# Gate tiles per pair of strips, transposes in groups of eight, and a new TensorE order in a two-stage attention and gated convolution

## The chip, the cores and the metric

The kernel runs on one core of a Trainium2 chip. The metric is the device time of one execution in microseconds (us). The time shown is the median of three executions; beside it stands one profiled execution with its own time and its own span (first to last instruction).

## What is computed

The input `x` has 4 batches of 12800 rows of 128 channels, and 32 inducing rows attend to it; then the rows of `x` attend to the 32 results. A gated layer follows: a causal convolution of five taps gives a gate, a 128x128 product gives a value, and a second 128x128 product makes the output.

```python
def mab(q, kv):
    s = scale * (q @ kv.transpose(0, 2, 1))
    s = s - s.max(-1, keepdims=True)
    a = np.exp(s)
    a /= a.sum(-1, keepdims=True) + 1e-09
    return a @ kv
h = mab(I, x)                    # (4, 32, 128)
y = mab(x, h)                    # (4, 12800, 128)
for k in range(5):
    gate_pre += conv_w[k] * yp[:, k:k + S, :]   # yp: y with 4 zero rows ahead
gate = 1 / (1 + exp(-gate_pre))
out = (gate * (y @ w_val)) @ w_out
```

## The kernel before

**Tiling.** The 12800 rows of a batch are four strips of 3200 (`R = 4`), and 4 x 32 inducing rows fill the 128 partitions. Along a strip the work goes in chunks: eight in batch 0 (128 to 512 columns a strip), seven in each other batch (`SIZES`). `x` comes in twice: with channels on the partitions (`xt`, which the scores read) and with rows on the partitions (`xk`, which the weighted sums read). In batch 0 only chunk 4 of `xk` is loaded; the others are made on the chip from `xt` by TensorE transposes (`make_xk`, lines 379 to 413). For the other batches `xk` is loaded.

**Stages of a batch**, with the names that the order table uses:
- `s1` (line 425): scores of the inducing rows in float32, each strip in its own 32 columns of the array. VectorE copies them to `ss` and keeps the maximum (433).
- `gm` (437): the maximum over the chunks of a group (`GROUPS`) and over the strips (GpSimd, 453 to 460).
- `x` (379): in batch 0, 128x128 transposes in groups of four into PSUM, copied to `xk` by ScalarE (406) or VectorE (408) as `XEV` says.
- `h` (489): the exponentials (ScalarE, 468), transposed by VectorE (473), times `xk`; VectorE adds the sums up in `H` (498, 500).
- `u`, `t`, `w`, `W` (`prep` to `prep3`): the groups are put together and divided (`hn`, 539), transposed (`hT`, 548 to 551), turned into the gate and value weights in two float16 halves, and spread for the four strips (624, then copies 632 and 634).
- `s2` (694): scores of `x` against `hT`, and the softmax over 32 through VectorE (700, 705, 723 to 726, 740), GpSimd (711, 734) and ScalarE (717), ending in two float16 halves, `P1` (745) and `P2` (752).
- `r` (`rblock`, 781): a half block of the gated layer. Half 0 of chunk k ends the gates of strips 0 and 1, makes the values of chunk k-1 for strips 2 and 3 and begins chunk k's gates there; half 1 ends the gates of strips 2 and 3, makes chunk k's values for strips 0 and 1 and begins chunk k+1's gates there. A strip's gate has 15 matmuls (766), its value three (775); each uses 32 rows of the array, and the four strips run side by side. ScalarE then makes the `tanh` of a pair's gates (834), VectorE multiplies with the values (844), ScalarE and GpSimd split the product in float16 halves `gh` (857) and `gl` (862).
- `o` (`outp`, 866): three matmuls make a strip's outputs (880 to 882); ScalarE (892) or VectorE (890) copies them to `os`, as `OUTV` says, and SyncE stores them (897). The last chunk has one float32 product (873) instead.
- `z` (916): matmuls of zeros that fill a wait; eight more stand at the very start (905).

**PSUM.** Half of its eight banks is `a`, four buffers of one bank for everything but gates and transposes. The other half is one tile, `gates`, of four banks: bank r holds strip r's gates, and the groups of transposes of `x` use the four banks in turn.

**What sets the order.** TensorE goes through `ORDER`, a written table of the names above, from the front to the back. `Plan.order` (79) gives every operation the time by which its users need it and lays the other engines' queues out greedily, with costs from `COST` and shifts from `URGE`; `PASSES` says how often. The result is emitted as it stands. SyncE issues every load and store in one queue, in that order. Buffers are counted in `BUFS`: four tiles `xk`, eleven `xt`, four `os`.

Of the kernel before, what the change touches and what calls it, by code (L numbers as in the profile page):

```python
# [12 lines left out]
F32 = mybir.dt.float32  # L13
# [24 lines left out]
PASSES = 6  # L38
# [174 lines left out]
def tile_kernel(ctx: ExitStack, tc: tile.TileContext, xt, xk, indT_in, w64, out):  # L213
# [11 lines left out]
    gates = psum.tile([P, R, 512], F32, name="gates")  # L225
# [92 lines left out]
    def pt(key, shape=(P, 512), dt=F32):  # L318
        if key[0][0] == "g":
            t = st[key] = gates[:, int(key[0][1:])]  # L320
            return t
        t = st[key] = psum.tile(list(shape), dt, name=key[0], tag=key[0], bufs=BUFS[key[0]])
        return t
# [29 lines left out]
    def load_xt(b, c, u=1):  # L353
        n = wid(b, c)
        o = R * (FIRST[b][c] + (HALO if c else 0))
        key, at = xt_of(b, c, u)
        own = key[2] == c

        def f():
            if own:  # L360
                sb(pxt, key, [P, 16, R, 32])
            first = at - (HALO // 32 if c == 0 else 0)
            nc.sync.dma_start(st[key][:, first:first + n // 32].rearrange("p i r q -> p (i r q)"), xt[b, :, o:o + R * n])

        ix["xt", b, c, u] = sp(n * 2048 / BW + 1.2 * ((b, c) == (0, 2) and ("xt", 0, 1, 1) in ix), f, [key] * own, [key] * (not own))
# [13 lines left out]
    def make_xk(b, c, eng):  # L379
# [13 lines left out]
        for g in range(0, n, 4):  # L393
            k = min(4, n - g)
            tk = (f"g{g // 4 % 4}", "tp", b, c, g)

            def tp(g=g, k=k, tk=tk):
                t = st[tk] = pt(tk).rearrange("p (i c) -> p i c", c=P)
# [4 lines left out]
            def ev(g=g, k=k, tk=tk, e=eng[g // 4 % len(eng)]):  # L403
# [6 lines left out]
            e = eng[g // 4 % len(eng)]  # L410
            i = PE(0.109 * k + 0.02, tp, [ix["xt", b, c, 1], i_const], [tk], [xkey], lag=0.22)
            last.append(op("ACT" if e == "S" else "DVE", 0.6 if e == "S" else 0.69, ev, [i, i0], 0.0, [], [tk, key]))
# [347 lines left out]
    def gate_mm(b, c, r, u):  # L760
        if u == 0:
            pt((f"g{r}", b, c))
# [3 lines left out]
        T.matmul(st[f"g{r}", b, c][:, :n], st["W", b][q, w, k, :], st[("P1", "P2")[e]][q, o:o + n],  # L766
# [11 lines left out]
    seqs = [(b, c) for b in range(B) for c in range(len(SIZES[b]))]  # L778
    split = begun(tuple(SIZES[b][c] for b, c in seqs), len(taps), EVEN)

    def rblock(k, half):
# [20 lines left out]
        def part(whole):  # L802

            todo, new, use, before = [], [], list(held), max(spent.values())
            while any(work.values()) and (whole or any(w and w[0][0] is val_mm for w in work.values())):
# [4 lines left out]
                key = ("a", "v", b, c, r) if fn is val_mm else (f"g{r}", b, c)  # L810
                if u == 0:
                    new.append(key)
                elif key not in new and key not in use:
                    use.append(key)
# [13 lines left out]
        if cur:  # L828
# [3 lines left out]
            def th(b=b, c=c, p=p, n=SIZES[b][c]):  # L832
                t = sb(pw, ("tg", b, c, p), [P, 2, 512])
                S.activation(t[:, :, :n], gates[:, 2 * p:2 * p + 2, :n], AF.Tanh, scale=st["gsc", b])  # L834

            ix["tg", b, c, p] = op("ACT", cost("act", 2 * SIZES[b][c]) + 0.06, th, [i, ix["gsc", b]], 0.0, [("tg", b, c, p)],
                                   [(f"g{r}", b, c) for r in ends] + [("gsc", b)])
# [28 lines left out]
    def outp(k, r):  # L866
# [3 lines left out]
        key, os = ("a", "o", b, c, r), ("os", b, c, r)  # L870
        if k == len(seqs) - 1:
# [37 lines left out]
    def idle(k, n):  # L909

        key = ("g3", "idle", k)

        def f():
            t = pt(key)
# [40 lines left out]
GROUPS = [[[0, 1, 2], [3, 4], [5, 6, 7]], [[0, 1, 2, 3], [4, 5, 6]], [[0, 1, 2], [3, 4, 5, 6]], [[0, 1, 2], [3, 4, 5, 6]]]  # L955
ORDER = [
# [40 lines left out]
]  # L997
XEV = ["SSSS", "SSSS", "SVSS", "SSSS", "SSVS", "SSSV", "SVSS", "SSSV"]
URGE = {
    "e1.f": 2.5,  # L1000
    "s2.sub": 6,
    "s2.hi": -18.5,
    "s2.lo": 3.5,
    "s2.tout": 0,
    "s2.ex": 3,
    "s2.tin": -5,
    "rblock.gv": -4.5,
    "s2.sm": -7,
# [73 lines left out]
```

## Time and profile before

| | |
|---|---|
| median of three executions | 299.47 us (297.91 to 300.87) |
| the profiled execution | 299.25 us, of which the span is 297.1 us |
| granted TensorE clock | 0.997 |
| TensorE matmuls busy | 281.7 us, 95% of the span |
| VectorE, ScalarE, GpSimd busy | 228.1, 209.1, 213.6 us |
| HBM read, written | 47.63 MB, 26.21 MB |

In the chain of waits each piece has a start, a length and what ran. A matmul's row has its start and a modelled end, so the pace of TensorE is read from start to start. A float32 matmul of the scores or the weighted sums shows as two records.

### The profile page before, as it was taken

How to read it: one execution, taken by the hardware profiler on the slowest of the kernel's cores; microseconds unless marked ns; L12 is line 12 of the kernel's file. 1: busy time of each engine (PE TensorE's matmuls, PEld its weight loads, DVE VectorE, ACT ScalarE, POOL GpSimd, SP SyncE). 2: the span in 40 equal slices, each digit the busy share in tenths (PEclk: the TensorE clock that was granted, in tenths of full speed). 3: DMA queues.
4: the chain of work that ended last, by engine and by line, in shares of the span. 5: the costliest groups of instructions: out<-in, count | busy, mean ns of one | idle time of the engine just before them, and what ended most of it. 6: DMA issues, size and time to landing. Idle time of an engine off the chain costs nothing.

```text
span 297.1 us, 10038 instructions
## 1 busy us (share of the span) xinstructions
PE 281.7 (95%) x4040; PEld 136.8 (46%) x4040; DVE 228.1 (77%) x569; ACT 209.1 (70%) x325; POOL 213.6 (72%) x256
## 2 busy tenths in 40 slices
PE   8787799999999999999999999999999999999993
PEld 3454544565433435563544544464444344433442
DVE  1245599999795999896888888899888996786550
ACT  2372606378776859797588856958789698878784
POOL 1020117796975897889768897599999999997570
PEclk9999999999999999999999999999999999999998
DMA  7949999699993789989999593705243324333355
GB/s 294 425 176 365 389 382 410 227 330 388 342 332 145 221 319 353 410 270 334 347 399 340 163 354 112 277 3 195 89 166 120 129 109 155 133 139 145 143 212 188
DMA packets 24382, 74.50 MB, mean 251 GB/s; under 512 B 2832, under 2 KB 12560, under 8 KB 22160
## 3 DMA queue, kind: packets, MB, share of 16 engines
q1 hardware_dynamic: 24192, 73.84, 67.5%
q8 instruction: 32, 0.52, 0.7%
q14 instruction: 14, 0.11, 0.1%
q10 hardware_dynamic: 144, 0.02, 0.0%
HBM read 47.63 MB, written 26.21 MB: 249 GB/s over the span
## 4 chain that ended last, share of the span: by engine, by line
PE 80%; ACT 8%; DMA 5%; issue 3%; DVE 2%; SPq 1%; ACTq 0%; DVEq 0%
PE gates L766 26%; PE a L880 7%; PE a L489 7%; PE a L694 7%; PE a L425 6%; PE a L881 6%; PE a L882 6%; PE a L775 5%; DMA xt<-in_xt_dram 5%; PE gates L401 4%; PE gates L916 3%; ACT tg L834 2%; ACT gh L857 2%; ACT xk L406 2%; ACT os L892 2%
## 5 line engine op out<-in xcount | busy, mean ns | idle before, releaser
L862 POOL TENSOR_TENSOR gl<-tg,gh 128x1024 f16<-128x1024 f32 (+4 forms) x56 | 106.3, 1904 | 17.1 <-ACT gh L857 12.4
L766 PE MATMUL gates<-P,W 32*128 32x448 f16 (+5 forms) x1740 | 109.5, 345 | 1.2 <-ACT tg L834 1.1
L834 ACT ACTIVATE tg<-gates,gsc 128x1024 f32<-128x1024 f32 (+5 forms) x58 | 57.8, 996 | 34.9 <-PE gates L766 34.0
L844 DVE SCALAR_TENSOR_TENSOR tg<-tg,a 128x512 f32<-128x512 f32 (+5 forms) x116 | 65.4, 603 | 15.9 <-PE a L775 13.9
L766 PEld LDWEIGHTS <-W 32*128 32x128 f16 x1740 | 53.2, 92 | 42.5 <-issue 13.6
L857 ACT CAST gh<-tg 128x1024 f16<-128x1024 f32 (+4 forms) x56 | 52.6, 944 | 1.1 <-PE a L881 0.8
L892 ACT ACTIVATE os<-a,osc 128x448 f32<-128x448 f32 (+5 forms) x75 | 44.7, 616 | 8.1 <-PE a L882 4.1
L775 PE MATMUL a<-P,W 32*128 32x512 f16 (+5 forms) x348 | 42.4, 348 | 0.0
L880 PE MATMUL a<-gh,wo 128*128 128x512 f16 (+4 forms) x112 | 40.2, 359 | 0.0
L881 PE MATMUL a<-gh,wo 128*128 128x512 f16 (+4 forms) x112 | 39.6, 354 | 0.0
L882 PE MATMUL a<-gl,wo 128*128 128x512 f16 (+4 forms) x112 | 39.5, 354 | 0.0
L890 DVE TENSOR_SCALAR os<-a,osc 128x512 f32<-128x512 f32 (+3 forms) x41 | 27.8, 688 | 9.9 <-PE a L882 9.7
L752 POOL TENSOR_TENSOR P<-pt,P 128x512 f16<-128x512 f32 (+4 forms) x29 | 29.8, 1034 | 3.9 <-ACT P L745 3.7
L711 POOL TENSOR_TENSOR e<-e,m 128x512 f32<-128x512 f32 (+4 forms) x29 | 27.0, 938 | 6.6 <-DVE m L705 6.5
L734 POOL TENSOR_TENSOR e<-e,z 128x512 f32<-128x512 f32 (+4 forms) x29 | 27.1, 938 | 4.0 <-DVE z L726 1.5
L433 DVE TENSOR_SCALAR_CACHE_REDUCE ss<-a 128x512 f32<-128x512 f32 (+5 forms) x29 | 17.5, 605 | 15.0 <-PE a L425 14.6
L425 PE MATMUL a<-xt,indT 128*32 128x512 f32 (+5 forms) x232 | 27.6, 546 | 0.9 <-DMA xt<-in_xt_dram 0.8
L489 PE MATMUL a<-xk,et 128*32 128x129 f32 x800 | 27.9, 275 | 0.0
L489 PEld LDWEIGHTS a<-xk,et 128*32 128x32 f32 x800 | 23.2, 109 | 7.5 <-issue 5.0
L694 PE MATMUL a<-xt,hT 128*32 128x512 f32 (+4 forms) x232 | 26.5, 545 | 0.0
L406 ACT COPY xk<-gates 128x512 f32<-128x512 f32 x18 | 10.1, 588 | 19.6 <-PE gates L401 19.6
L880 PEld LDWEIGHTS <-wo 128*128 128x128 f16 x112 | 10.9, 97 | 26.7 <-issue 19.4
(103 smaller groups left out, 328.4 us busy)
## 6 DMA issues: line engine op xcount, KB each, us to landing
xt<-in_xt_dram SPq DMA_DIRECT2D x11, 1024.0 KB, 8.9
out_dram<-os SPq DMA_DIRECT2D x40, 256.0 KB, 2.8
xk<-in_xk_dram SPq DMA_DIRECT2D x10, 903.0 KB, 6.9
out_dram<-os SPq DMA_DIRECT2D x40, 224.0 KB, 3.5
xt<-in_xt_dram SPq DMA_DIRECT2D x8, 896.0 KB, 8.6
xk<-in_xk_dram SPq DMA_DIRECT2D x6, 1032.0 KB, 6.8
xt<-in_xt_dram SPq DMA_DIRECT2D x6, 960.0 KB, 7.7
xk<-in_xk_dram SPq DMA_DIRECT2D x5, 967.5 KB, 6.5
```

The costliest lines, as they stand in the source:

```text
L489: T.matmul(t[32 * s:32 * s + 32, :P + 1], e[:, 32 * i:32 * i + 32], x[:, m + i, :], start=i < R, stop=i >= nb - R)
L694: T.matmul(s[32 * r:32 * r + 32, :n], st["hT", b], x[:, m:m + nb, r, :], start=True, stop=True)
L766: T.matmul(st[f"g{r}", b, c][:, :n], st["W", b][q, w, k, :], st[("P1", "P2")[e]][q, o:o + n], start=u == 0, stop=u == len(taps) - 1)
L775: T.matmul(st["a", "v", b, c, r][:, :n], st["W", b][q, w, TAPS, :], st[("P1", "P2")[e]][q, o:o + n], start=u == 0, stop=u == 2)
L834: S.activation(t[:, :, :n], gates[:, 2 * p:2 * p + 2, :n], AF.Tanh, scale=st["gsc", b])
L844: V.scalar_tensor_tensor(t, t, 1.0, st["a", "v", b, c, r][:, :n], ALU.add, ALU.mult)
L857: S.copy(sb(pw, g1, [P, 2, 512], F16)[:, :, :n], st[tg][:, :, :n])
L862: G.tensor_tensor(sb(pw, g2, [P, 2, 512], F16)[:, :, :n], st[tg][:, :, :n], st[g1][:, :, :n], ALU.subtract)
L880: T.matmul(t, w[:, 0], st[g1][:, q, :n], start=True, stop=False)
L881: T.matmul(t, w[:, 1], st[g1][:, q, :n], start=False, stop=False)
L882: T.matmul(t, w[:, 0], st[g2][:, q, :n], start=False, stop=True)
L892: S.activation(o, a, AF.Copy, scale=st["osc", b])
```

## The change

- The four-bank tile `gates` goes. In its place stand two tiles from the pool, `g0` and `g1`, of two banks each, one buffer each: `g0` holds the gates of strips 0 and 1, `g1` those of strips 2 and 3. `tanh` reads a whole tile.
- The transposes of `x` go in groups of eight, alternately into `g0` and `g1`, with one copy of up to 1024 columns per group: 11 copies (9 on ScalarE, 2 on VectorE) instead of 21 (18 and 3).
- The outputs of the last two chunks go to the tiles `et`, `pt` and `ss`, which the scores used, instead of `os`.
- The tables are new: `ORDER`, `GROUPS[0]`, `XEV`, `URGE`, `OUTV` (47 of 116 output copies on VectorE, 41 before), `EVEN` (how evenly the gates are shared between two half blocks), `AHEAD` and `PASSES`. Of `z` there are 31 where there were 33.

```diff
-    gates = psum.tile([P, R, 512], F32, name="gates")
...
     def pt(key, shape=(P, 512), dt=F32):
-        if key[0][0] == "g":
-            t = st[key] = gates[:, int(key[0][1:])]
-            return t
...
-        for g in range(0, n, 4):
-            k = min(4, n - g)
-            tk = (f"g{g // 4 % 4}", "tp", b, c, g)
+        for g in range(0, n, 8):
+            k = min(8, n - g)
+            tk = (f"g{g // 8 % 2}", "tp", b, c, g)
...
-                t = st[tk] = pt(tk).rearrange("p (i c) -> p i c", c=P)
+                t = st[tk] = pt(tk, (P, 1024)).rearrange("p (i c) -> p i c", c=P)
...
     def gate_mm(b, c, r, u):
-        if u == 0:
-            pt((f"g{r}", b, c))
+        if (f"g{r // 2}", b, c) not in st:
+            pt((f"g{r // 2}", b, c), (P, 2, 512))
...
-        T.matmul(st[f"g{r}", b, c][:, :n], st["W", b][q, w, k, :], st[("P1", "P2")[e]][q, o:o + n],
+        T.matmul(st[f"g{r // 2}", b, c][:, r % 2, :n], st["W", b][q, w, k, :], st[("P1", "P2")[e]][q, o:o + n],
...
-                S.activation(t[:, :, :n], gates[:, 2 * p:2 * p + 2, :n], AF.Tanh, scale=st["gsc", b])
+                S.activation(t[:, :, :n], st[f"g{p}", b, c][:, :, :n], AF.Tanh, scale=st["gsc", b])
...
         key, os = ("a", "o", b, c, r), ("os", b, c, r)
+        if k >= len(seqs) - 2:
+            os = ("ss" if k == len(seqs) - 1 else ("et", "et", "et", "pt")[r], "out", b, c, r)
...
 ORDER = [
-    ("s1", 0, 0), ("z", 4, 3), ("z", 1, 6), ("x", 0, 0), ("s1", 0, 2), ("x", 0, 2), ("s1", 0, 1), ("x", 0, 1),
+    ("z", 0, 3), ("l", 0, 0), ("s1", 0, 0), ("x", 0, 0), ("s1", 0, 1), ("z", 1, 6), ("gm", 0, 0), ("x", 0, 1),
...
-EVEN = 0.02
+EVEN = 0.04765998428116873
```

The order of the built program shows three places on TensorE. Lines are about three lower in the changed kernel (397 for 401, 422 for 425, 763 for 766, 772 for 775), and 881 to 883 stand for 880 to 882.

The first is chunk 2 of batch 0, whose 16 transposes stand in four groups before:

```order
L401 MATMUL gates<-identf,xt 128x128 [waits Activation_49]
L401 MATMUL gates<-identf,xt 128x128 x7
L401 MATMUL gates<-identf,xt 128x128 [waits Activation_49]
L401 MATMUL gates<-identf,xt 128x128 x3
L401 MATMUL gates<-identf,xt 128x128 [waits DVE_49]
L401 MATMUL gates<-identf,xt 128x128 x3
L425 MATMUL a<-xt,indT 32x256 [waits DMAHW3_49]
```

and now in two, where the second waits for no other engine's copy:

```order
L397 MATMUL g_198<-identf,xt 128x128 [waits Activation_49]
L397 MATMUL g_198<-identf,xt 128x128 x7
L397 MATMUL g_212<-identf,xt 128x128 [waits PE_49]
L397 MATMUL g_212<-identf,xt 128x128 x7
L422 MATMUL a<-xt,indT 32x512 [waits DMAHW4_49]
```

The waits for ScalarE and VectorE in the middle of a chunk are gone.

The second is a half block late in batch 3. Before, the first gate matmul after the output matmuls waits for ScalarE:

```order
L882 MATMUL a<-gl,wo 128x512 [waits Pool_49]
...
L880 MATMUL a<-gh,wo 128x512 [waits DVE_49]
...
L766 MATMUL gates<-P_96,W 128x512 [waits Activation_49]
...
L775 MATMUL a<-P_95,W 128x512 [waits DVE_49]
```

and now the half block opens with values, and only the first gate matmul of a new chunk waits for ScalarE, twelve matmuls in:

```order
L883 MATMUL a<-gl,wo 128x512 [waits Pool_49]
...
L881 MATMUL a<-gh,wo 128x512 [waits DVE_49]
...
L772 MATMUL a<-P_94,W 128x512 [waits DVE_49]
...
L763 MATMUL g_5420<-P_94,W 128x512 [waits Activation_49]
```

The wait moved from the start of the half block to the place where a gate tile is written anew.

The third is the end of the program. Before, the last values and the last float32 products close it:

```order
L882 MATMUL a<-gl,wo 128x512 [waits Pool_49]
...
L775 MATMUL a<-P_95,W 128x160 [waits Activation_49]
...
L873 MATMUL a<-tg,wof 128x160 [waits DVE_49,Activation_49]
L873 MATMUL a<-tg,wof 128x160 [waits DVE_49]
```

and now the values and the small products stand ahead of the last outputs of the chunk with 512 columns:

```order
L772 MATMUL a<-P_94,W 128x160 [waits DVE_49]
...
L874 MATMUL a<-tg,wof 128x160 [waits DVE_49] x3
L874 MATMUL a<-tg,wof 128x160 [waits Activation_49]
...
L883 MATMUL a<-gl,wo 128x512 [waits Pool_49]
...
L881 MATMUL a<-gh,wo 128x512 [waits DVE_49]
```

What moved is the last thing stored: four strips of 160 columns before, a strip of 512 columns now.

More of the change, by code (lines that the diff above doesn't have):

```diff
@@ L37 @@
 SCALE = 1.0 / math.sqrt(P)
-PASSES = 6
+PASSES = 2
 LAT = dict(PE=0.3, DVE=0.06, ACT=0.045, POOL=0.09, SP=0.05, NOP=0.0)
@@ L363, in f @@
             nc.sync.dma_start(st[key][:, first:first + n // 32].rearrange("p i r q -> p (i r q)"), xt[b, :, o:o + R * n])
-        ix["xt", b, c, u] = sp(n * 2048 / BW + 1.2 * ((b, c) == (0, 2) and ("xt", 0, 1, 1) in ix), f, [key] * own, [key] * (not own))
+        ix["xt", b, c, u] = sp(n * 2048 / BW, f, [key] * own, [key] * (not own))
     def load_xk(b, c):
@@ L401, in tp, with ev @@
                     T.transpose(t[:, i, :], x[:, o + g + i].rearrange("p r q -> p (r q)"), c_["identf"])
-            def ev(g=g, k=k, tk=tk, e=eng[g // 4 % len(eng)]):
+            def ev(g=g, k=k, tk=tk, e=eng[g // 8 % len(eng)]):
                 dst, src = st[key][:, m + g:m + g + k, :P], st[tk][:, :k, :]
@@ L408, in ev @@
                     V.tensor_copy(dst, src)
-            e = eng[g // 4 % len(eng)]
+            e = eng[g // 8 % len(eng)]
             i = PE(0.109 * k + 0.02, tp, [ix["xt", b, c, 1], i_const], [tk], [xkey], lag=0.22)
-            last.append(op("ACT" if e == "S" else "DVE", 0.6 if e == "S" else 0.69, ev, [i, i0], 0.0, [], [tk, key]))
+            last.append(op("ACT" if e == "S" else "DVE", cost("act", 128 * k) - 0.03 if e == "S" else cost("psum", 128 * k) + 0.02,
+                           ev, [i, i0], 0.0, [], [tk, key]))
         ix["xk", b, c] = op("NOP", 0.0, lambda: None, last)
@@ L778, in tile_kernel @@
     seqs = [(b, c) for b in range(B) for c in range(len(SIZES[b]))]
+    made = set()
     split = begun(tuple(SIZES[b][c] for b, c in seqs), len(taps), EVEN)
@@ L809, in part @@
                 spent[r] += COST["unit"] * SIZES[b][c]
-                key = ("a", "v", b, c, r) if fn is val_mm else (f"g{r}", b, c)
-                if u == 0:
+                key = ("a", "v", b, c, r) if fn is val_mm else (f"g{r // 2}", b, c)
+                if u == 0 and key not in made:
                     new.append(key)
+                    made.add(key)
                 elif key not in new and key not in use:
@@ L833, in th @@
                 t = sb(pw, ("tg", b, c, p), [P, 2, 512])
-                S.activation(t[:, :, :n], gates[:, 2 * p:2 * p + 2, :n], AF.Tanh, scale=st["gsc", b])
+                S.activation(t[:, :, :n], st[f"g{p}", b, c][:, :, :n], AF.Tanh, scale=st["gsc", b])
             ix["tg", b, c, p] = op("ACT", cost("act", 2 * SIZES[b][c]) + 0.06, th, [i, ix["gsc", b]], 0.0, [("tg", b, c, p)],
-                                   [(f"g{r}", b, c) for r in ends] + [("gsc", b)])
+                                   [(f"g{p}", b, c), ("gsc", b)])
         if val:
@@ L909, in idle @@
     def idle(k, n):
-        key = ("g3", "idle", k)
+        key = ("g1", "idle", k)
         def f():
-            t = pt(key)
+            t = pt(key, (P, 2, 512))[:, 0]
             for _ in range(n):
@@ L952, in tile_kernel @@
     return plan
-GROUPS = [[[0, 1, 2], [3, 4], [5, 6, 7]], [[0, 1, 2, 3], [4, 5, 6]], [[0, 1, 2], [3, 4, 5, 6]], [[0, 1, 2], [3, 4, 5, 6]]]
+GROUPS = [[[0, 1], [2, 3, 4], [5, 6, 7]], [[0, 1, 2, 3], [4, 5, 6]], [[0, 1, 2], [3, 4, 5, 6]], [[0, 1, 2], [3, 4, 5, 6]]]
 ORDER = [
[40 rows of a table removed]
[40 rows of a table added]
 ]
-XEV = ["SSSS", "SSSS", "SVSS", "SSSS", "SSVS", "SSSV", "SVSS", "SSSV"]
+XEV = ["SSSV", "SVSS", "SVSS", "SSSV", "SSSS", "SSVS", "SVSS", "SSVS"]
 URGE = {
[L1000 to L1008, printed above, removed]
-    "make_xk.ev": 0.5,
-    "h.acc": -3,
-    "halves.lo": -1.5,
-    "s2.mx": 11.5,
-    "s1.g": -3.5,
-    "s2.nm": -3.5,
-    "halves.hi": -1.5,
-    "e1.tr": -1.5,
-    "evac.ev": -6.5,
-    "rblock.th": -1,
-    "values.gv": -11.5,
-    "rows.th": 0.5,
-    "gmax.f1": 2,
-    "gmax.f0": 8.5,
-    "outp.ev": -1.5,
+    "e1.f": -13,
+    "s2.sub": 8,
+    "s2.hi": -28,
+    "s2.lo": 7.5,
+    "s2.tout": -6.5,
+    "s2.ex": 1.5,
+    "s2.tin": -3.5,
+    "rblock.gv": -5,
+    "s2.sm": -2.5,
+    "make_xk.ev": 1.5,
+    "h.acc": -4,
+    "halves.lo": -1,
+    "s2.mx": 5.5,
+    "s1.g": -5.5,
+    "s2.nm": -3,
+    "halves.hi": -2,
+    "e1.tr": -4.5,
+    "evac.ev": -20.5,
+    "rblock.th": 8,
+    "values.gv": -4,
+    "rows.th": -8,
+    "gmax.f1": 4,
+    "gmax.f0": 1,
+    "outp.ev": 4,
 }
 TURNED = (0,)
-EVEN = 0.02
+EVEN = 0.04765998428116873
 OUTV = [
[3 rows of a table removed]
[4 rows of a table added]
 ]
@@ L1033 @@
 WARM = 8
-AHEAD = 30
+AHEAD = 19
 AGAIN = [(), (), (), ()]
 BUFS = dict(xt=11, wf=2, cg=2, hn=2, wof=1, xk=4, ss=4, et=3, e=3, pt=2, tg=3, gh=2, gl=2, q=2, qm=2, tq=2, osc=2, os=4, H=4, mx=2, ng=2, m1=2, f=2, D=6, hT=2,
-            gmx=2, vmx=2, gsc=2, wo=2, w2=2, W=2, m2=3, z=3, a=4, g0=1, g1=1, g2=1, g3=1)
+            gmx=2, vmx=2, gsc=2, wo=2, w2=2, W=2, m2=3, z=3, a=4, g0=1, g1=1)
 def kernel(**inputs):
```

85 rows, old and new, of tables (ORDER, OUTV) are left out of this document.

## The prediction

> **What bounds the kernel now.** I read the page's busy table first, then the shares of the chain of waits, then single stretches start to start.
>
> ```profile
> span 297.1 us, 10038 instructions
> PE 281.7 (95%) x4040; PEld 136.8 (46%) x4040; DVE 228.1 (77%) x569; ACT 209.1 (70%) x325; POOL 213.6 (72%) x256
> PE 80%; ACT 8%; DMA 5%; issue 3%; DVE 2%; SPq 1%; ACTq 0%; DVEq 0%
> ```
>
> TensorE is the bound: 95% busy, and 80% of the chain. Its idle time is 297.1 - 281.7 = 15.4 us. But a matmul's row has a modelled end that reaches over the next start, so I take its pace from starts. The timeline of TensorE late in batch 3:
>
> ```profile
> 261.73 0.48 PE L694 MATMUL a<-xt,hT 128*32 128x160 f32 x8
> 262.14 0.39 PE L880 MATMUL a<-gh,wo 128*128 128x512 f16 x1
> ...
> 272.73 0.39 PE L880 MATMUL a<-gh,wo 128*128 128x512 f16 x1
> ...
> 273.82 0.38 PE L882 MATMUL a<-gl,wo 128*128 128x512 f16 x1
> 274.13 0.39 PE L775 MATMUL a<-P,W 32*128 32x512 f16 x2
> ...
> 275.98 0.39 PE L880 MATMUL a<-gh,wo 128*128 128x512 f16 x1
> ```
>
> Five steps between output matmuls take 273.82 - 272.73 = 1.09, so 512 columns stream in 0.217 us. Six would be 1.30, yet the next half block starts after 1.40: changing the way the array is split costs about 0.11. The half block's 32 matmuls, four side by side, are eight steps, 1.73, and take 1.85: 0.12. The chain of waits early in batch 0 gives the strips' price and the first real stalls:
>
> ```profile
> 7.81 0.99 PE a L425 x8
> 8.80 1.04 PE gates L401 x8
> ...
> 9.86 0.59 ACT xk L406
> ...
> 10.50 0.67 PE gates L401 x4
> ...
> 11.27 0.70 DVE xk L408
> ...
> 12.02 0.67 PE gates L401 x4
> ...
> 12.71 1.08 ACT xk L406 x2
> ```
>
> Eight score records of 512 columns take 0.99, eight of 160 took 0.41 (261.73 to 262.14); the slope leaves 0.14 for the change. With these paces over the order of the program, the kernel before streams 248.1 us in 184 stretches, 22.3 us of changes; TensorE's last matmul ends at about 293, so some 21 us are true stalls, more than the idle column shows. Some 12 of them lie ahead of the first gate matmul.
>
> The Trainium skill, "Trainium Kernel Development and Optimization", Best Practices, says to judge headroom by LDWEIGHTS busy and not by matmul busy. By it (46% against 95%) the busy row would hide much more than 15 us; the starts agree in kind, with 21 us.
>
> **The change part by part: the start.** The fence above is chunk 2. The first copy (9.86) begins when all eight transposes of two groups are through, though it reads the first four; the third group (10.50) begins when that copy ends, the fourth (12.02) when VectorE's ends. No bank is short: there are four. The one tile makes them wait for each other.
>
> ```profile
> L401 PE MATMUL gates<-identf,xt 128*128 128x128 f32 x84 | 12.4, 282 | 6.7 <-ACT xk L406 4.7 <-DVE xk L408 2.1
> L406 ACT COPY xk<-gates 128x512 f32<-128x512 f32 x18 | 10.1, 588 | 19.6 <-PE gates L401 19.6
> L834 ACT ACTIVATE tg<-gates,gsc 128x1024 f32<-128x1024 f32 (+5 forms) x58 | 57.8, 996 | 34.9 <-PE gates L766 34.0
> ```
>
> A chunk of 16 takes 12.69 - 8.80 = 3.89, where 16 at 0.108 (eight in 0.87 between starts) and one change are 1.84: 2.05 lost, four times in batch 0, 8 us (the idle column has 6.7). With two tiles the second eight go on while the first are copied. A copy of 1024 columns is not in the trace: from 0.59 (512 columns) to 2 x 0.59, and I take 1.0, as the tanh row of 1024 columns has; on VectorE 0.70 to 1.4, I take 1.2. Both end before the next chunk of transposes, since scores of 0.86 to 1.9 us stand between. Is something else late next?
>
> ```profile
> 40.52 0.34 DVE hn L539
> ...
> 45.99 2.91 PE gates L916 x13
> ...
> 49.69 2.26 PE gates L916 x10
> ...
> 52.95 0.44 PE gates L766 x12
> ```
>
> The first gate matmul starts at 52.95 = 1.2 + 36.3 of streaming + 26 changes at 0.125 (3.3) + 12.1 of stalls: 8 in the transposes, 1.8 in the eight slow first matmuls below, 2.3 elsewhere. In the change's order 37.1 of streaming (14 more matmuls of `h` of batch 1, two fewer fillers) and 20 changes (2.5) stand ahead of it. With 1.2, the 1.8 and the 2.3 that is 44.9, and I add 0.6 for waits at the copies: 45.5, a gain of 7.4. For its cover:
>
> ```profile
> 21.67 0.33 SPq L374 DMA_DIRECT2D xk<-in_xk_dram  x1
> ...
> GB/s 294 425 176 365 389 382 410 227 330 388 342 332 145 221 319 353 410 270 334 347 399 340 163 354 112 277 3 195 89 166 120 129 109 155 133 139 145 143 212 188
> ```
>
> Loads: SyncE stood until 21.67 because chunk 4's `xk` was the fifth of four tiles, and the third slice fell to 176 GB/s. Now it is the third tile, does not wait, and stands ahead of chunk 5's `xt` and the weights (`raw`). The 7.7 MB up to the end of batch 0 need, at 294 GB/s in the first 7.4 us and 425 after, until 20.3 us; by the sum above TensorE wants the last, chunk 5, at about 22. The mask and weight chain from `hT` to the first 160 columns of `P2` is, by the durations of its instructions in the new queues, 8 us, from 34.7 to 42.8, ahead of 45.5. I take -7.0. Bounds: -4 (loads or the chain cost three) and -9.
>
> The fillers:
>
> ```profile
> 1.17 3.59 PE L905 MATMUL a<-zero 128*128 128x512 f16 x8 [1.17 <-DVE warm L241]
> ...
> 5.25 2.12 PE L916 MATMUL gates<-zero 128*128 128x512 f16 x9
> ```
>
> The first eight step by 0.44, the nine after 5.25 by 0.22. Three fillers now stand right behind the eight, 0.65 us at the fast step and 1.3 at the slow one, largely inside the wait for the first loads; 0 to +0.7, I take 0. "TensorE: Matmul & The Clock Gate", HAM oscillation, in the Trainium skill, says that an idle gap over about 3.4 us halves the clock again. By it a start with fewer fillers could lose 1.7 us more; here no gap was that long, and the granted clock is 1.00 in every window below.
>
> **The body.** Behind the first gate matmul stand 210.6 us of streaming (211.8 before), 33 strip stretches (40), 58 of rows (60) and 59 full (58): -1.2 - 7 x 0.14 - 2 x 0.12 + 0.11 = -2.3.
>
> ```profile
> L766 PE MATMUL gates<-P,W 32*128 32x448 f16 (+5 forms) x1740 | 109.5, 345 | 1.2 <-ACT tg L834 1.1
> ```
>
> Gates waited 1.1 us for `tanh`; the wait now stands twelve matmuls later. 0 to -1.1, I take -0.5. What is late next is VectorE. The table by stage:
>
> ```profile
> 0.00:41.00 41.00, 32.68 (x395) 19.11 (x396) 18.61 (x62) 16.67 (x32) 5.81 (x33) 1.00 0.84 332
> 41.00:53.00 12.00, 11.99 (x135) 4.70 (x137) 11.47 (x40) 5.28 (x11) 8.00 (x17) 1.00 0.97 394
> 53.00:125.00 72.00, 71.49 (x1176) 35.87 (x1172) 63.03 (x168) 51.85 (x84) 58.27 (x76) 1.00 0.85 307
> 125.00:205.00 80.00, 78.83 (x1233) 38.71 (x1236) 69.35 (x169) 61.57 (x99) 66.53 (x73) 1.00 0.73 260
> ```
>
> The third pair of numbers is VectorE: 45% busy to 41, then 96%, then 88%. In a shorter start it has less time for the same work, and the new order puts work of batches 1 and 2 and output copies earlier: up to the gating products of chunk 7, half 0, its instructions sum to 99.0 us (90.7 before), and 72.4 of them come after the first `P` transpose is out, at about 41.5. So it is there at 113.9 at best, where TensorE, by its own sum, is at 110.0 and the products normally end 1.3 later: VectorE is 2.6 late, at the worst point 3.1. Values hold two of the four `a` buffers until then, so TensorE waits: +2.9. Bounds: 0 (outputs are read a half block later) and +12.9 (rival below). ScalarE loses six output copies of some 0.6 us and has the room.
>
> **The tail.**
>
> ```profile
> 282.89 0.39 PE L880 MATMUL a<-gh,wo 128*128 128x512 f16 x1
> ...
> 286.15 4.22 POOL L862 TENSOR_TENSOR gl<-tg,gh 128x1024 f16<-128x1024 f32 x2 [0.85 <-PE a L881]
> ...
> 291.41 0.38 PE L775 MATMUL a<-P,W 32*128 32x160 f16 x6
> ...
> 292.36 0.78 PE L873 MATMUL a<-tg,wof 128*128 128x160 f32 x4 [0.57 <-DVE tg L844]
> ```
>
> GpSimd's last half ends at 290.37, 7.5 after the last wide half block (282.89), and then four output matmuls, six value matmuls, a product on VectorE and four small records followed, to 293.1. The new order does the values and small matmuls while GpSimd works: after +7.5 come four matmuls (0.87), a copy of 512 columns (0.69) and a store.
>
> ```profile
> out_dram<-os SPq DMA_DIRECT2D x40, 256.0 KB, 2.8
> ...
> out_dram<-os SPq DMA_DIRECT2D x4, 80.0 KB, 1.8
> ```
>
> The store lands in 2.8 instead of 1.8. The small copies ended at 294.3, 2.8 ahead of the end, so: 7.5 + 0.9 + 0.8 + 3.8 = 13.0 after 282.89 instead of 14.2. I take -1.0, between -2 and +1. The other tiles for the outputs cost nothing: they are free by then.
>
> **Sum.** -7.0 - 2.3 - 0.5 + 2.9 - 1.0 = -7.9 against the profiled execution's 299.25 (span 297.1 and 2.15 around it): 291.4 us. The median of the runs, 299.47, is 0.2 above it.
>
> **Rivals.**
> - *VectorE costs nothing.* The products come late but nobody wants them: +0 for +2.9, 288.5. For it: outputs stand a half block (3.4 us) behind the products. Against it: the four buffers.
> - *The start doesn't get shorter*, because the copies still wait for both tiles or the loads and masks set the time. Then VectorE has its slack too: 299.25 - 2.3 - 0.5 - 1.0 = 295.5. For it: DMA is 84% busy up to 41. Against it: the waits in the fence end within 0.05 of copies, and SyncE's wait was for a tile.
> - *VectorE and TensorE go in lock step, slower.* Place: from 41.5 to the products of chunk 7. If VectorE idles 12.5% there, as from 53 to 125 (63.03 of 72), its 72.4 us take 82.7 and it is there at 124.2, 12.9 behind 111.3: 299.25 - 10.8 + 12.9 = 301.4. From 10.4% idle on it is slower than before. Against it: most of that idle time was a wait for TensorE, which would now be ahead.
>
> **How the numbers follow.** The forecast, 288 to 294, 0.60; VectorE free 0.13; the start as it was 0.14; lock step 0.08; the rest, such as loads of a later batch that come late, 0.05. About 1% is what a measurement of this kernel can tell from no change. The first two are faster by more; of the third a quarter comes within 1%, of the lock step half is slower. Faster 0.85, same 0.08, slower 0.07. The range goes from -9 at the start with free VectorE (286.5) to a start that stays and a little loss (297).
>
> **What would show it.** Right: the first gate matmul near 45.5; chunks of 16 transposes in about 1.85 start to start; SyncE's first `xk` load issued below 10 us; VectorE over 93% busy from 41 to 105; the last small products ahead of the last outputs. Wrong: first gates after 50, or TensorE waiting for VectorE or for `xt` for more than 6 us in all between 50 and 160.

## The result and the profile after

The changed kernel takes 289.15 us (median of four executions, 288.69 to 289.56), the kernel before, run beside it, 299.75: a ratio of 0.9652 with a 95% interval of 0.96 to 0.9703. The forecast was 291.4 in a range of 286.5 to 297.0. One execution among all that follow, the profiled one of `e5_load_after`, ran at a granted clock of 0.754 and took 357 us; all others ran at 0.99 to 1.00. The profiled execution of the changed kernel took 288.69 with a span of 286.6, 10.5 less than before, where the sum had 7.9. From the page of the changed kernel, the span, the busy row and the shares of the chain:

```profile
span 286.6 us, 10022 instructions
PE 278.0 (97%) x4038; PEld 136.0 (47%) x4038; DVE 230.4 (80%) x574; ACT 204.6 (71%) x310; POOL 214.2 (75%) x256
PE 90%; DVE 4%; DMA 3%; issue 0%; SPq 0%; ACT 0%
```

TensorE has nearly the same work (4038 matmul records for 4040) and 90% of the chain instead of 80%. The start comes next, as the chain of waits from 0 to 60 and, for the last row, TensorE's timeline:

```profile
15.55 1.90 PE g L397 x16
...
19.54 1.90 PE g L397 x16
...
24.43 1.90 PE g L397 x16
```

```profile
46.14 1.02 PE L763 MATMUL g<-P,W 32*128 32x128 f16 x42
```

The last three chunks of 16 transposes take 1.90 each with the change of the array's split, the first, chunk 2, takes 1.84 by TensorE's timeline (3.89 before). None of them waits, and the first gate matmul stands at 46.14 instead of 52.95. SyncE's timeline and the page's row of transfer rates answer for the loads:

```profile
4.12 1.39 SPq L370 DMA_DIRECT2D xk<-in_xk_dram  x1
```

```profile
GB/s 250 408 418 421 415 387 365 414 392 395 361 314 234 403 274 294 413 363 267 239 160 234 342 387 109 106 125 159 88 132 130 129 148 128 156 146 148 189 159 194
```

Chunk 4's rows are asked for at 4.12 (21.67 before), and no slice of the start falls to 176 GB/s. For the body, the table by stage (VectorE is the third pair) and the row of the gates:

```profile
46.00:114.00 68.00, 67.56 (x1100) 32.67 (x1100) 65.48 (x170) 49.20 (x79) 59.41 (x73) 1.00 0.93 343
```

```profile
L763 PE MATMUL g<-P,W 32*128 32x448 f16 (+5 forms) x1740 | 109.7, 345 | 0.0
```

VectorE is busy for 65.48 of 68.00, 96% (over 93% was forecast, from 41 to 105), and gates wait for no `tanh`. From the first gate matmul to the end of the last wide half block the kernel takes 272.05 - 46.14 = 225.9, before 282.89 - 52.95 = 229.9. Last the tail, on TensorE, ScalarE and SyncE:

```profile
272.05 0.39 PE L881 MATMUL a<-gh,wo 128*128 128x512 f16 x1
...
277.89 1.48 PE L874 MATMUL a<-tg,wof 128*128 128x160 f32 x8
...
280.93 0.38 PE L883 MATMUL a<-gl,wo 128*128 128x512 f16 x1
```

```profile
281.35 0.69 ACT L893 ACTIVATE et<-a,osc 128x512 f32<-128x512 f32 x1 [0.61 <-PE a L883]
```

```profile
278.80 0.33 SPq L898 DMA_DIRECT2D out_dram<-et  x1
279.23 2.81 SPq L898 DMA_DIRECT2D out_dram<-ss  x4
282.13 0.38 SPq L898 DMA_DIRECT2D out_dram<-et  x1
282.61 0.38 SPq L898 DMA_DIRECT2D out_dram<-pt  x1
283.08 0.41 SPq L898 DMA_DIRECT2D out_dram<-et  x1
```

The last copy ends at 282.04, its store is issued only at 283.08. The tail is 286.6 - 272.05 = 14.5, before 297.1 - 282.89 = 14.2. So the 10.5 us are 6.8 in the start and 4.0 in the body, less 0.3 given back in the tail.

### The profile page after: what moved, and what is told of

It is laid out like the page before. It is cut to its first block, busy times and chain, and to the rows that moved or that the text cites. A ratio compares the mean times of both kernels' runs of the same rounds, so it can differ in the third digit from the quotient of the medians.

```text
span 286.6 us, 10022 instructions
## 1 busy us (share of the span) xinstructions
PE 278.0 (97%) x4038; PEld 136.0 (47%) x4038; DVE 230.4 (80%) x574; ACT 204.6 (71%) x310; POOL 214.2 (75%) x256
## 4 chain that ended last, share of the span: by engine, by line
PE 90%; DVE 4%; DMA 3%; issue 0%; SPq 0%; ACT 0%
PE g L763 29%; PE a L881 10%; PE a L486 8%; PE a L691 8%; PE a L883 7%; PE a L882 7%; PE a L772 7%; PE a L422 7%; PE g L397 3%; DMA xt<-in_xt_dram 3%; PE g L917 2%; PE a L621 1%; DVE ss L430 1%; DVE e L697 1%; PE a L528 1%; PE a L874 0%
## 5 line engine op out<-in xcount | busy, mean ns | idle before, releaser
L763 PE MATMUL g<-P,W 32*128 32x448 f16 (+5 forms) x1740 | 109.7, 345 | 0.0
L833 ACT ACTIVATE tg<-g,gsc 128x1024 f32<-128x1024 f32 (+5 forms) x58 | 57.8, 996 | 29.4 <-PE g L763 24.9
L763 PEld LDWEIGHTS <-W 32*128 32x128 f16 x1740 | 50.6, 92 | 43.2 <-issue 13.1
L893 ACT ACTIVATE os<-a,osc 128x512 f32<-128x512 f32 (+4 forms) x63 | 38.1, 633 | 5.5 <-PE a L883 5.3
L891 DVE TENSOR_SCALAR os<-a,osc 128x448 f32<-128x448 f32 (+4 forms) x45 | 29.6, 674 | 7.8 <-PE a L883 7.4
L714 ACT ACTIVATE e<-e 128x512 f32<-128x512 f32 (+4 forms) x29 | 16.5, 576 | 10.5 <-POOL e L708 10.4
```

What stands on the lines that cost most here:

```text
L763: T.matmul(st[f"g{r // 2}", b, c][:, r % 2, :n], st["W", b][q, w, k, :], st[("P1", "P2")[e]][q, o:o + n], start=u == 0, stop=u == len(taps ...
L833: S.activation(t[:, :, :n], st[f"g{p}", b, c][:, :, :n], AF.Tanh, scale=st["gsc", b])
```

## The experiments

Each is compared with the kernel before on the same chip: the ratio is to that kernel timed beside it, whose median lay between 298.94 and 300.78. The table gives the median, the ratio and its interval, and from the profile the first gate matmul, the body (to the end of the last wide half block), the tail and the span, all in us. The first gate is read from TensorE's timeline, which has 52.88 for the kernel before where the chain has 52.95.

| kernel | median | ratio (95%) | first gate | body | tail | span |
|---|---|---|---|---|---|---|
| before | 299.47 | | 52.9 | 230.0 | 14.2 | 297.1 |
| the change | 289.15 | 0.9652 (0.9600 to 0.9703) | 46.1 | 225.9 | 14.5 | 286.6 |
| e1_one_tile | 291.40 | 0.9710 (0.9663 to 0.9757) | 46.5 | 229.2 | 14.8 | 290.5 |
| e2_old_tables | 289.67 | 0.9658 (0.9609 to 0.9708) | 45.4 | 227.0 | 14.8 | 287.2 |
| e3_old_tiles | 296.55 | 0.9891 (0.9837 to 0.9946) | 52.1 | 227.3 | 15.4 | 294.7 |
| e4_late_load | 291.01 | 0.9693 (0.9617 to 0.9769) | 49.3 | 225.6 | 15.2 | 290.2 |
| e5_load_after | 302.27 | 1.0097 (1.0068 to 1.0125) | | | | |
| e6_load_before | 312.55 | 1.0456 (1.0416 to 1.0495) | 53.5 | 243.4 | 14.9 | 311.8 |
| e7_copy_on_act | 288.51 | 0.9649 (0.9627 to 0.9671) | 45.7 | 225.2 | 15.2 | 286.1 |
| e8_two_queues | 288.50 | 0.9655 (0.9636 to 0.9674) | 45.9 | 225.8 | 15.0 | 286.6 |
| e9_load_after_psum | 291.05 | 0.9698 (0.9652 to 0.9743) | 45.7 | 227.9 | 14.5 | 288.2 |
| e10_load_before_psum | 300.88 | 1.0036 (1.0009 to 1.0064) | 52.9 | 231.8 | 15.1 | 299.7 |
| e11_tail_act | 287.80 | 0.9598 (0.9553 to 0.9642) | 46.8 | 225.6 | 13.9 | 286.3 |
| e12_tail_os | 289.44 | 0.9649 (0.9612 to 0.9686) | 45.8 | 225.8 | 16.8 | 288.4 |

Kernels that share a start differ by up to 1.1 in the first gate from one profile to the next (45.7 in e7_copy_on_act, 46.8 in e11_tail_act); smaller differences there mean nothing. The body and the tail come from one profile of each kernel.

**One tile again, groups of eight kept (`e1_one_tile`).**

```diff
+    gates = psum.tile([P, 2, 1024], F32, name="gates")
...
     def pt(key, shape=(P, 512), dt=F32):
+        if key[0][0] == "g":
+            t = gates[:, int(key[0][1:])]
+            t = st[key] = t.rearrange("p (a b) -> p a b", a=2) if len(shape) == 3 else t
+            return t
```

> The changed kernel, with one tile of four banks in place of the two gate tiles: groups of eight transposes stay, in its halves, and so does the order of TensorE. If it is the size of the groups that freed the transposes, only the copies start later (both wait for all 16 transposes of a chunk): in the changed kernel the next chunk's transposes come 3 us behind or more, except for chunk 7 (1.0 us behind chunk 6), so the first gate matmul comes 0.5 to 1.5 later than 46.1 and the time is 289.5 to 291. If it is the second tile that freed them, each of four chunks loses its 2.05 us again, the first gate matmul comes at 52 to 54 and the time is 295 to 297.

The timeline of TensorE, from chunk 3 to chunk 7, and ScalarE's two copies of chunk 3:

```profile
14.83 1.97 PE L402 MATMUL gates<-identf,xt 128*128 128x128 f32 x16 [0.51 <-DVE xk L409]
...
18.81 1.97 PE L402 MATMUL gates<-identf,xt 128*128 128x128 f32 x16
...
23.83 1.97 PE L402 MATMUL gates<-identf,xt 128*128 128x128 f32 x16
...
27.81 0.44 PE L402 MATMUL gates<-identf,xt 128*128 128x128 f32 x2 [1.00 <-ACT xk L407]
```

```profile
16.83 1.93 ACT L407 COPY xk<-gates 128x1024 f32<-128x1024 f32 x2 [3.31 <-PE gates L402]
```

Sixteen transposes go through in one stretch with one tile too, and chunk 7 waits the expected 1.00. So groups of eight free the transposes without a second tile. The tile still ties the groups together: the copies start at 16.83, when the sixteenth transpose is through (14.83 + 1.97). But a chunk of 16 is now two groups, and no third one stands behind a copy, as the groups at 10.50 and 12.02 did in the kernel before. Two tiles with groups of four were not run, so whether the second tile alone would have freed them is open. In the start the second tile is worth little. The body is 3.3 longer in this profile: three half blocks lose 0.4 more each (the waits page has gates waiting for `tanh` again, 0.7 in two of them), and 1.7 is a wait for a load of `xk`, issued at 131.78 instead of 129.53 because SyncE stood with a store ahead of it. Whether this last wait belongs to the one tile or to that execution stays open. In time the second tile is not shown to be worth anything: the median is 2.3 higher, and the intervals overlap.

**New tiles with old tables (`e2_old_tables`), and old tiles with new tables (`e3_old_tiles`).** The first has the changed functions and, word for word, the old `GROUPS`, `ORDER`, `XEV`, `URGE`, `OUTV`, `EVEN`, `AHEAD` and `PASSES`; the second the reverse. Some of the first's edits, against the changed kernel:

```diff
-AHEAD = 19
+AHEAD = 30
-PASSES = 2
+PASSES = 6
...
-EVEN = 0.04765998428116873
+EVEN = 0.02
```

> The changed kernel's tiles, groups of eight and last output tiles, with all tables of the kernel before (order, groups, copies' engines, URGE, EVEN, OUTV, AHEAD, PASSES). If the tiles and groups bring the start's gain and the tables the body's: first gate matmul at 45.5 to 47.5 (8 us of transpose stalls gone from 52.95, less what the late load of chunk 4 costs), from there 230 to the end of the last wide half block and 14.2 behind it as before, 291.5 to 294 in all. If the tables bring the start's gain (the early load and the order of the first scores): first gate matmul after 50 and 296 or more.

> The kernel before (one gate tile, groups of four transposes, outputs in their own tiles to the end), with all tables of the changed kernel. If tiles and groups bring the start's gain: the waits inside four chunks come back, 2.05 us each, first gate matmul at 52 to 54; behind it the body takes 226 as in the changed kernel, so 294 to 297 in all. If the order of the table brings it: first gate matmul at 46 to 48.5 and 289 to 291.5.

TensorE and SyncE in the kernel with the old tables:

```profile
8.97 1.97 PE L397 MATMUL g<-identf,xt 128*128 128x128 f32 x16
...
14.31 1.97 PE L397 MATMUL g<-identf,xt 128*128 128x128 f32 x16
...
23.09 1.97 PE L397 MATMUL g<-identf,xt 128*128 128x128 f32 x16
```

```profile
17.60 0.33 SPq L370 DMA_DIRECT2D xk<-in_xk_dram  x1
```

and TensorE's waits in the one with the old tiles:

```profile
PE gates L401 <- ACT xk L406: 4.5, 7, 0.7
```

Tiles and groups alone give 9.9 of the 10.5 us of span, the tables alone 2.4, both together 0.6 more than the tiles. In time, the ratios of 0.9658 (tiles alone) and 0.9652 (both) can't be told apart: that the new tables add to the new tiles is not shown, and on the old tiles they are worth about 1%. The start is settled: 45.4 and 46.1 with new tiles under the old and the new table, 52.1 with old ones under the new table, whose transposes wait 4.5 us for ScalarE again. The body is not a sum: 230.0 before, 227.0 with the new tiles, 227.3 with the new tables, 225.9 with both. TensorE's order is the old one with the new tiles too, so what they save there are waits, 1.1 of them the gates' for `tanh`. Of what the new tables save, some 1.8 are less streaming and fewer changes of split (an estimate from the matmuls of both traces, at 0.217 for 512 columns and 0.11 to 0.14 a change). Why the two together save 4.1 and not 5.7 stays open. In the old order the load of chunk 4 is still issued late, at 17.60, and no sum waits for it.

**The early load (`e4_late_load`).**

```diff
-    ("s1", 0, 4), ("k", 0, 4), ("s1", 0, 3), ("x", 0, 3), ("gm", 0, 1), ("h", 0, 1), ("s1", 0, 7), ("h", 0, 0),
-    ("s1", 0, 6), ("l", 0, 5), ("x", 0, 6), ("h", 0, 4), ("raw",), ("h", 0, 2), ("s1", 0, 5), ("gm", 0, 2),
+    ("s1", 0, 4), ("s1", 0, 3), ("x", 0, 3), ("gm", 0, 1), ("h", 0, 1), ("s1", 0, 7), ("h", 0, 0),
+    ("s1", 0, 6), ("l", 0, 5), ("x", 0, 6), ("k", 0, 4), ("h", 0, 4), ("raw",), ("h", 0, 2), ("s1", 0, 5), ("gm", 0, 2),
```

> The changed kernel with one entry of its order moved: the load of chunk 4's rows stands right ahead of the sums that need it, as in the kernel before, so its tile is again one that must first come free, and SyncE waits there with the weights and the last scores' input behind it. If the early load was part of the start's gain: SyncE stands until 20 us or later, the sums of chunk 4 or the scores of chunks 6 and 7 wait, and the first gate matmul comes 2 to 4 us later, 291 to 293 in all. If the load had cover anyway (the waits at the transposes were all of the start's loss): within 0.7 of 46.1 and 289 to 290.

SyncE, and TensorE's waits up to 50:

```profile
18.20 0.33 SPq L370 DMA_DIRECT2D xk<-in_xk_dram  x1
```

```profile
PE a L486 <- DMA xk<-in_xk_dram: 2.5, 1, 2.5
```

The load is issued at 18.20, the sums wait 2.5 us for it, and the first gate matmul stands at 49.3, 3.2 later. The median is 1.9 above the changed kernel's, with overlapping intervals. So the early load is what the new order needs, since it asks for chunk 4's sums early; it is no gain of its own, as the old order without it starts as early.

**VectorE loaded, first attempt (`e5_load_after`, `e6_load_before`).** Both kernels got 28 copies that nobody needs:

```diff
                     V.scalar_tensor_tensor(t, t, 1.0, st["a", "v", b, c, r][:, :n], ALU.add, ALU.mult)
+                    if seqs.index((b, c)) < 7:
+                        V.tensor_copy(c_["junk"], c_["zero"].bitcast(F32))
```

> The changed kernel with one more instruction on VectorE behind each of the 28 gating products of chunks 0 to 6: a copy of 128x256 float32 numbers into a tile that nobody reads (work added, nothing left out). At some 0.3 us each (transposes of 256 columns take 0.31) that is 8 us more between 46 and 114, where VectorE is idle for 2.5 of 68 us. If VectorE sets the pace of that stretch, as the forecast's term of 2.9 us has it: the products of chunk 7, half 0, end 5 to 8 later than 115.2 and the time is 294 to 297. If its work still has cover (products late, but nobody waits): under 2 later and 289 to 291.

> The kernel before with the same 28 copies on VectorE. There it is idle for some 12% from 53 to 125, 7 to 8 us up to the products of chunk 7, half 0 (120.9). If that idle time is slack, as the forecast had it when it charged the shorter start with a VectorE lag: the 8 us vanish in it and the time is 299.5 to 301.5. If VectorE was in the pace of the kernel before as well, its idle time being waits for TensorE at each half block: +4 to +8, 303 to 308.

The timeline of VectorE and of GpSimd in the kernel before with these copies:

```profile
99.37 0.28 DVE L847 COPY junk<-zero 128x256 f32<-128x256 f32 x1
...
103.56 1.92 DVE L847 COPY junk<-zero 128x256 f32<-128x256 f32 x1
105.40 0.68 DVE L845 SCALAR_TENSOR_TENSOR tg<-tg,a 128x512 f32<-128x512 f32 x1
106.00 1.63 DVE L847 COPY junk<-zero 128x256 f32<-128x256 f32 x1
```

```profile
103.19 4.29 POOL L865 TENSOR_TENSOR gl<-tg,gh 128x1024 f16<-128x1024 f32 x2 [1.71 <-ACT gh L860]
```

The price was wrong: 0.28 us where GpSimd is idle, up to 1.92 where it works, 21.1 us in all instead of 8. The two long copies end at 105.5 and 107.6, GpSimd's two instructions at about 105.3 and 107.5. The kernel before became 13.6 longer, the changed one 13.1 (13.8 against the 288.5 of the next two kernels, timed beside it). Of 21.1 us the kernel before hid 7.5, about the idle time that its expectation had counted on (7 to 8). What the changed kernel hid can't be said: its only profile is of the execution of 357 us, where the copies sum to 16.9. By that it hid 3.1 to 3.8, by 21.1 us 7.3 to 8.0; its expectation had 2.5 of idle time. So this pair leaves the changed kernel's price open.

**VectorE loaded, second attempt (`e9_load_after_psum`, `e10_load_before_psum`)**, with a source in PSUM:

```diff
+                    if seqs.index((b, c)) < 7:
+                        V.tensor_copy(c_["junk"], st["a", "v", b, c, r][:, :128])
```

> As the run with 28 added VectorE copies in the changed kernel, but each now reads 128 columns of the value tile in PSUM (so that it doesn't stand while GpSimd works, which made the other copies 0.28 to 1.92 us) and writes a tile that nobody reads. At 0.2 to 0.25 us each that is 6 to 7 us. VectorE is idle for 2.5 us of the 68 from 46 to 114. If each us of its work there counts: +3.5 to +4.5 on the changed kernel, 292.7 to 293.7. If what it is late is made up later or hidden in the half block between product and output: under +1.5, 289.2 to 290.7.

> The same 28 copies of 128 columns from PSUM in the kernel before, where VectorE is idle for 7.5 us from 53 to the products of chunk 7, half 0. If that is slack, 6 to 7 us vanish in it: 299 to 300.5. If it is idle at times that can't be used (each half block waits for it in turn): +3 or more, 302.5 and up.

The row of the copies and the table by stage, first of the changed kernel with them, then of the kernel before:

```profile
L846 DVE COPY junk<-a 128x128 f32<-128x128 f32 x28 | 7.9, 281 | 0.0
```

```profile
46.00:114.00 68.00, 66.49 (x1048) 31.69 (x1044) 66.82 (x191) 47.96 (x76) 57.40 (x72) 1.00 0.91 338
```

```profile
L847 DVE COPY junk<-a 128x128 f32<-128x128 f32 x28 | 7.9, 281 | 0.0
```

```profile
53.00:125.00 72.00, 70.50 (x1152) 36.08 (x1152) 66.34 (x192) 50.14 (x80) 56.61 (x68) 1.00 0.84 300
```

The same 7.9 us cost about the same in both. The end of the last wide half block comes 1.6 later in the changed kernel (272.05 to 273.62) and 1.8 later in the kernel before (282.89 to 284.65). Counted from the first gate matmul, which stands 0.4 earlier in the first of the two, the body is 2.0 and 1.8 longer. The products of chunk 7, half 0, end 2.3 and 2.7 later, 2.7 in both when counted from the first gate, and some of that is made good behind them. The spans grow by 1.6 and 2.6, the medians by 1.6 to 1.9 (against 289.44 of e12_tail_os, timed beside it, and 289.15) and by 1.1. For the changed kernel the intervals of the ratios overlap, so there it is the trace that shows the price. Neither of the alternatives expected is met: VectorE's work isn't free in the kernel before, and it isn't at full price in the changed one, though its idle share there is 4% and not 12%.

**The wait behind the scores at 12.5 (`e7_copy_on_act`).** In the changed kernel's profile the scores that begin at 12.48 are cut in two by a wait for VectorE, which empties the bank only behind chunk 2's second copy:

```profile
14.49 1.06 PE L422 MATMUL a<-xt,indT 128*32 128x512 f32 x8 [0.94 <-DVE ss L430]
```

That copy goes to ScalarE:

```diff
-XEV = ["SSSV", "SVSS", "SVSS", "SSSV", "SSSS", "SSVS", "SVSS", "SSVS"]
+XEV = ["SSSV", "SVSS", "SSSS", "SSSV", "SSSS", "SSVS", "SVSS", "SSVS"]
```

> The changed kernel with the second 1024-column copy of chunk 2 on ScalarE instead of VectorE. The scores at 12.5 wait 0.9 us for a bank that VectorE reads only behind this copy. If that copy is what is late: this wait goes, ScalarE's two copies end at 13.7, still ahead of chunk 3's transposes, the first gate matmul comes 0.8 to 1.0 earlier than 46.14, and the time is 288.0 to 288.6. If the wait is made good elsewhere (the loads or the exponentials on ScalarE then hold it up): first gate within 0.3 and 289.

The wait is gone, and the first gate stands 0.5 earlier. But in the profile of the last experiment, `e12_tail_os`, whose start is the changed kernel's to the letter, the scores go through as well:

```profile
12.70 1.92 PE L422 MATMUL a<-xt,indT 128*32 128x512 f32 x16
```

So the wait of 0.9 was one execution's, the edit is worth nothing that this run shows, and a ratio of 0.9649 against 0.9652 agrees.

**Stores on a second queue (`e8_two_queues`, `e11_tail_act`).** Two of the last stores from ScalarE, then all three wide ones (the second kernel also has the edit of `XEV`):

```diff
-            nc.sync.dma_start(out[b, :, r, FIRST[b][c]:FIRST[b][c] + n], st[os][:, :n])
+            q = nc.scalar if k == len(seqs) - 2 and r and not v else nc.sync
+            q.dma_start(out[b, :, r, FIRST[b][c]:FIRST[b][c] + n], st[os][:, :n])
```

```diff
-            q = nc.scalar if k == len(seqs) - 2 and r and not v else nc.sync
+            q = nc.scalar if k == len(seqs) - 2 and r else nc.sync
```

> The changed kernel with two of its last eight stores issued by ScalarE, right behind its own copies, instead of by SyncE: the two wide strips that ScalarE copies last. In the changed kernel the last copy ends at 282.04, yet its store is issued only at 283.08, since SyncE goes through eight stores one behind another. If SyncE's row is what ends the tail: the last store is issued at 282.1 to 282.3, and the time from the end of the last wide half block (272.05) to the end is 13.5 to 13.9 instead of 14.55; 288.2 to 288.7 in all. If landing sets the end whoever issues: 14.3 to 14.6 and 289.

> The changed kernel with two edits: chunk 2's second copy of 1024 columns on ScalarE, and the last three wide strips stored by ScalarE instead of SyncE. SyncE's issue of the last small store stood for 1.3 to 2.3 us in every profile so far, with the wide ones behind it. With them on ScalarE that stand only holds up small stores: the last wide store is issued 0.8 behind ScalarE's last copy, the tail from 272.05 on takes 14.0 instead of 14.55, the scores' wait at 12.5 is gone (0.5 to 0.8), together 287.5 to 288.3. If the landing of the small stores or the DMA engines set the end: the tail stays at 14.5 and only the start's 0.5 is left, 288.3 to 288.8.

SyncE's timeline with two moved, then SyncE's and ScalarE's with three:

```profile
278.80 3.81 SPq L899 DMA_DIRECT2D out_dram<-ss  x4
282.71 0.41 SPq L899 DMA_DIRECT2D out_dram<-pt  x1
```

```profile
279.57 2.50 SPq L899 DMA_DIRECT2D out_dram<-ss  x4
```

```profile
281.69 0.69 ACT L893 ACTIVATE et<-a,osc 128x512 f32<-128x512 f32 x1 [0.61 <-PE a L883]
281.83 0.34 ACTq L899 DMA_DIRECT2D out_dram<-pt  x1
282.41 0.34 ACTq L899 DMA_DIRECT2D out_dram<-et  x1
```

With two moved the tail wins nothing (15.0): one of the four small stores takes 2.28 us to issue, and `pt` stands behind it until 282.71. With three moved, the last wide store is issued 0.03 behind its copy, and the tail takes 13.9, the shortest of all profiles of this order (14.5 to 15.2 in the others, without e12_tail_os). The time, 287.80, is the lowest of all kernels, 0.5% under the changed kernel's; the intervals overlap, so that it beats the kernel before is shown, and that it beats the change is not.

**The last outputs in their own tiles (`e12_tail_os`).**

```diff
-        if k >= len(seqs) - 2:
+        if False:
             os = ("ss" if k == len(seqs) - 1 else ("et", "et", "et", "pt")[r], "out", b, c, r)
```

> The changed kernel with the outputs of the last two chunks in their own four tiles again, as in the kernel before. If those tiles were free by then, as the forecast had it: within 0.4 of the changed kernel, 288.8 to 289.5, and no copy of an output waits for a store. If the tail needs more than four: a copy waits for a store that lands 2.4 to 3.2 behind its issue, the tail is 1 to 2 longer, 290 to 291.

```profile
ACT os L893 <- DMA out_dram<-os: 4.0, 1, 4.0
```

In its profile (waits from 276 on) a copy waits 4.0 us for a store to land, and the tail is 2.3 longer, 16.8. The median is only 0.3 above the changed kernel's: the profiled execution, 290.11, was the longest of its six. That the borrowed tiles take a wait away is shown for that execution; what they are worth in time is not.

## Why the prediction was right, and where it was not

**The start, -7.0: measured -6.8.** The four stalls of 2.05 are gone, the copies of 1024 columns take 1.01 on ScalarE and 1.22 on VectorE (taken: 1.0 and 1.2), and the loads and the weight chain come in time. One reason in it was half wrong: "With two tiles the second eight go on while the first are copied" names the second tile, and e1_one_tile shows that groups of eight do it in one tile as well.

**The body, +0.1 in the sum: measured -4.0.** The failed step is "+2.9", VectorE. Its reading of VectorE holds: the products of chunk 7, half 0, were forecast at 113.9 and end at 115.2, 62.4 us behind those of chunk 0. That TensorE then waits for it does not show. From 41 to 130 TensorE's waits page has 0.2 us for VectorE:

```profile
PE a L486 <- DVE tg L843: 0.2, 1, 0.2
```

By streaming and changes of split, TensorE does lose something up to there, 2.1 us in the changed kernel, most of it between 50 and 60 and not near chunk 7. But the kernel before loses 1.8 in its own stretch, with 12% of VectorE idle (both are estimates, from the first gate to 1.3 ahead of the products' end, at 0.217 for 512 columns). The sum was made against a time that already held this loss, and charged it again. What had to go in was the difference of the two, about nothing. With that the sum gives 288.5, the first rival's time, and its reason holds in part: of 7.9 us more on VectorE, 1.8 to 2.0 came through in either kernel, and the rest did not. What causes the loss itself is not shown. Idle time of 12% did not mean more slack than 4%.

One figure of the prediction's working doesn't come out of its rows. At the pace that it shows, 0.217 for 512 columns, the kernel before streams 252 us and not 248.1, and its stalls are 17 us and not 21. The sums of streaming fit 0.213. Differences between the two kernels hardly change by it, but "+2.9" compared VectorE with an absolute time of TensorE: 110.0 would have been 111, and about 1 us of the lag goes with it.

The other terms of the body fit: -2.3 for streaming and changes and -1.1 for `tanh` leave 0.6 of the 4.0 without a cause. Waits for `tanh` fell from 1.1 to 0 (taken: 0.5, bound 1.1); e1_one_tile and e3_old_tiles, with one tile, have 0.7 of them, so that much is the second tile's share. Of the 2.3 for streaming and changes, 0.8 was only work moved ahead of the first gate, which the start paid for; the 14 stretches fewer are worth 1.7 at 0.12 each. Under the same tiles TensorE's last matmul begins 1.4 earlier in the new order than in the old one (280.9 for 282.4), and the span ends 0.6 earlier.

**The tail, -1.0: measured +0.3.** GpSimd ends 7.3 behind the last wide half block (taken: 7.5). Then nine matmuls follow and not four, so the last copy ends 10.0 behind it instead of 9.2. And the store was taken as issued at once: SyncE issues eight stores one behind another at 0.45 each, one of them stands for 1.34, and the last leaves 1.04 behind its copy. From there to the end 3.5 pass (taken: 3.8). That is 0.8 + 1.0 - 0.3 = 1.5 more than forecast. e11_tail_act takes the queue out of it and has 13.9.

**The rivals.** That the start stays as it was is refuted by the first gate at 46.14, and e2_old_tables has the gain without the tables. The lock step needed 10.4% of idle VectorE from 41.5 to chunk 7; there is 4%.

## What to carry to other kernels

When an engine looks like the next bound, compute what it costs in the kernel as it is by the same rule before charging it to the new one; only the difference belongs in the sum. Load the suspect engine with a known dose in both kernels: the share of it that comes through in the time is its price, and the idle share in the profile is not. A queue that issues transfers is serial as well: at the end of a program count its issues, not only the landing of the last one.

## What the runs showed of the hardware that was not expected

A float32 copy on VectorE from SBUF to SBUF, 256 columns, takes 0.28 us alone and up to 1.92 while a GpSimd instruction runs; the long ones end some 0.15 behind that instruction. A copy of 128 columns from PSUM takes 0.27 to 0.29 each time, beside GpSimd or not. The Trainium skill, "SBUF — State Buffer", Terms, says that VectorE and GpSimd share a pair of SBUF ports, locked for a whole instruction, and that the loser "fully blocks"; the rows above agree.

SyncE's issue of a store, 0.33 to 0.45 us as a rule, took 1.34 at 280.70 in the changed kernel, 2.28 at 279.3 with two stores on ScalarE and 0.94 at 290.7 in the kernel before. In all three a packet of the queue that the profile calls instruction was read at that moment; the stretch from 280.5 to 282.2 of the changed kernel:

```profile
q8 instruction: 1, 0.02, 3.4%
```

The changed kernel has 32 such packets of 16 KB, and each of its six issues of over 0.9 us behind the first loads begins within 0.9 us of one. In the kernel before only five of nine such issues do (those at 124.33, 141.92, 156.94 and 171.68 do not), so there is at least one other cause. That a packet holds up an issue was not tried.
